# Full-array maxima in the lead, a strip mask made by ScalarE, and narrower score strips in a transformer-block kernel

## The chip, the cores and the metric

The kernel runs on one core of one Trainium2 chip, in one launch. What is measured is the device time of that core in microseconds (us), from the first to the last instruction with what lies around them. The engines in the text are TensorE (PE in the profile, with its weight loads as PEld), VectorE (DVE), ScalarE (ACT), GpSimd (POOL) and the queue that issues most DMAs (SP).

## The reference

A block of a sequence model: layer norm and sliding-window attention, a residual sum, then layer norm and a gated mixer over the sequence, and a second residual sum. Only the attention half is touched here. Sizes are S = 2048 positions, D = 640, 32 heads of 20, and a window of 256 keys.

```
q, k, v = split(layernorm(x) @ wqkv)            # 32 heads, Dh = 20
scores  = q @ k.T * Dh**-0.5
mask    = (i - j >= 0) & (i - j < 256)          # query i, key j
p       = softmax(where(mask, scores, -1e9))
h       = x + (p @ v) @ wo
z       = gelu(layernorm(h) @ w_in); z1, z2 = halves of z
out     = h + (z1 * (w_sp @ layernorm(z2) + b_sp)) @ w_out
```

## The kernel before

Positions are cut into 16 tiles of 128. The kernel runs through these stages, one behind the other:

- **V stage.** For each tile: layer norm of x (statistics on DVE, the variance plus epsilon and its power of -0.5 on POOL, lines 75 and 76, the normalizing on DVE, line 79), transposes on PE (line 394), a split of the result into a rounded high part and the rest, and the product with the weights for v (lines 410 to 412: high by high, high by low, low by high). The weights are split too: high parts by ACT (line 459), low parts by DVE and POOL (line 460).
- **Q/K stage.** 40 items (`qk_item`, 10 weight blocks m by 4 position chunks c), each of 5 steps of 3 matmuls of 512 columns (lines 434 to 436). A finished item is split into three bf16 parts (lines 440 to 443: ACT, DVE, ACT, POOL) and stored. The first 24 items run alone. The other 16, "dense" in the code, are a generator that yields after each step of 3 matmuls.
- **Lead.** The last 48 and more dense steps alternate with `max_item`s of head group 0 and the first of group 1. A `max_item` computes 128 queries by their keys for one head, to find each query's largest score: four matmuls of 32 queries each, side by side in four column strips of the array (line 278), each over its own 288 keys; then DVE adds a mask and takes the maximum (line 284). `strip` is that mask for query tiles from 2 on, the same pattern in each 32 partitions; `mask` serves tiles 0 and 1.
- **Main loop.** 128 units u (8 groups of 4 heads by 16 key tiles), 130 steps. Step s issues, for each of 4 heads hh, the `max_item` of unit s + 20 and the `score_item` of unit s: 128 keys by up to 384 queries, four strips of 32 keys, each over the same 384 queries (line 332), into one of three PSUM banks `s2`; ACT takes the exponential of the whole 128x384 (line 335). Behind hh = 2 comes the `pv_item` of unit s - 2 (line 356), in f32, which first had POOL clear what lies outside the window (lines 337 and 340). Every fourth pv ends with a copy from PSUM by ACT (line 366). At four steps ahead of a new head group `max_rows` sends the maxima through DRAM (m_d, lines 297 and 299) into the rows that the group's first scores read. From unit 109 on there are no maxima left, and scores go two heads at a time into other banks.
- **Mixer.** Output projection, second layer norm and the gated mixer. The diff does not touch it.

PE, DVE and ACT run in the order in which the code is written. POOL and SP are ordered by a scheduler. In the prologue, POOL has to make the constants (`ident`, `half`, `mask`, `strip`, the ones in `v_sb`) and its share of line 460, and between them lies the power that the first normalized tile waits for.

The strip mask is made so before:

```
strip = tmp2.tile([P, 288], BF16, name="strip")
nc.gpsimd.memset(strip, 0.0)
for j in range(4):
    m = strip[32 * j:32 * j + 32]
    nc.gpsimd.affine_select(out=m, ... pattern=[[1, 288]], base=-1, channel_multiplier=-1, ...)
    nc.gpsimd.affine_select(out=m, ... pattern=[[-1, 288]], base=256, channel_multiplier=1, ...)
```

## Time and profile before

| | |
|---|---|
| time, three runs | 1188.43, 1192.71 (median), 1193.15 us |
| the profiled execution's own time | 1185.69 us |
| its span, first to last instruction | 1184.0 us |
| mean granted TensorE clock in it | 0.991 |
| PE busy | 1126.5 us (95%), 10272 matmuls |
| PEld, DVE, ACT, POOL busy | 963.8, 738.8, 537.6, 391.5 us |
| prologue, up to the first v matmul | 12.6 us |
| V stage to about 94 us, Q/K alone to about 196 us, lead to about 265 us, main loop to about 510 us | |

The ends of matmuls are modelled in this profile, so the start times of PE rows carry more than their durations: the distance from one group of matmuls to the next is what PE really took. "xN" merges N instructions of one kind that follow each other. In a row of a timeline the numbers are the start and the length in us; in square brackets stands how long the engine had been idle and what ended that. Rows of line 278 are maxima, of 332 scores, of 356 pv, of 434 to 436 dense Q/K steps.

### The profile page before, as it was taken

What the parts mean: (1) busy time and instruction counts of PE and PEld (TensorE: products, weight loads), DVE (VectorE), ACT (ScalarE), POOL (GpSimd) and SP (SyncE); (2) the same over time, 40 slices, a digit from 0 to 9 for tenths busy, and PEclk for the clock granted to TensorE, in tenths of its full rate; (3) what the DMA queues carried; (4) which work ended last, traced back from release to release, by engine and by line L of the source; (5) the groups of instructions that cost most, each with busy time, mean ns of one, the idle gap of its engine ahead of it and who ended that gap; (6) DMA issues with size and microseconds to landing.
All of it is one profiled execution on the core that took longest, in us unless ns stands there. A gap on an engine that the chain in (4) does not pass through costs nothing. (4 is left out here: it accounts for less than half of the span.)

```text
span 1184.0 us, 26538 instructions
## 1 busy us (share of the span) xinstructions
PE 1126.5 (95%) x10272; PEld 963.8 (81%) x10272; DVE 738.8 (62%) x1949; ACT 537.6 (45%) x1121; POOL 391.5 (33%) x485
## 2 busy tenths in 40 slices
PE   5999999999999999878899999899999899999998
PEld 5998886546666666468899999799999889999998
DVE  5541123658888888559967658755548985656443
ACT  3333433228888888834446655433335531221110
POOL 4123443336556555845722036100015530000000
PEclk9999999999999999989999999899999999999999
DMA  6212453543444441558845441133331364444322
GB/s 191 77 34 89 143 195 138 187 150 114 173 166 175 174 175 42 188 174 289 270 156 189 174 134 36 36 132 131 120 139 57 125 193 152 129 140 136 86 87 82
DMA packets 72125, 165.20 MB, mean 140 GB/s; under 512 B 9128, under 2 KB 33448, under 8 KB 70056
## 3 DMA queue, kind: packets, MB, share of 16 engines
q1 hardware_dynamic: 69696, 158.27, 40.1%
q10 hardware_dynamic: 2304, 5.24, 1.1%
q8 instruction: 80, 1.31, 0.5%
q14 instruction: 45, 0.37, 0.1%
HBM read 108.83 MB, written 54.66 MB: 138 GB/s over the span
## 5 line engine op out<-in xcount | busy, mean ns | idle before, releaser
L335 ACT ACTIVATE pt<-st 128x384 f32<-128x384 f32 (+2 forms) x474 | 199.0, 513 | 34.8 <-PE st L332 27.3
L284 DVE CUSTOM_DVE_ANT_0 junk<-sm,strip 128x288 bf16<-128x288 f32 x448 | 181.0, 454 | 50.8 <-PE sm L278 49.6
L930 PE MATMUL g<-zl,aw 128*128 128x432 f32 x768 | 173.6, 361 | 7.2 <-ACT zl L598 4.9
L598 ACT ACTIVATE aw<-fx 128x512 fp32r<-128x512 f32 (+2 forms) x160 | 92.9, 596 | 185.7 <-PE g L930 120.9
L930 PEld LDWEIGHTS g<-zl,aw 128*128 128x128 f32 x768 | 144.6, 189 | 15.3 <-ACT zl L598 5.7
L930 PE MATMUL g<-ze,aw 128*128 128x432 f32 x576 | 137.0, 365 | 4.1 <-DVE row L592 1.8
L592 DVE TENSOR_TENSOR aw<-fx,aw 128x512 fp32r<-128x512 f32 (+2 forms) x152 | 108.4, 722 | 36.2 <-ACT aw L598 36.0
L930 PEld LDWEIGHTS g<-ze,aw 128*128 128x128 f32 x576 | 108.8, 192 | 11.6 <-ACT aw L598 1.7
L332 PE MATMUL st<-slot 123*32 123x384 bf16 (+2 forms) x1536 | 110.6, 318 | 6.6 <-ACT pt L335 3.6
L337 POOL TENSOR_SCALAR_AFFINE_SELECT pt<-pt 128x512 f32<-128x512 f32 x128 | 82.1, 642 | 90.9 <-ACT pt L335 90.9
L278 PE MATMUL sm<-slot 120*32 120x288 bf16 (+2 forms) x1536 | 109.1, 284 | 3.2 <-DVE mcol L284 2.5
L356 PE MATMUL pv<-pt,v_sb 128*32 128x384 f32 (+2 forms) x1408 | 102.7, 384 | 3.0 <-POOL pt L340 1.9
L969 PE MATMUL out_ps<-wout,y_sp 128*128 128x320 f32 (+1 forms) x630 | 96.2, 309 | 0.4 <-ACT y_sp L122 0.4
L834 PE MATMUL zb<-win,aw 128*128 128x432 f32 x480 | 95.3, 359 | 0.0
L969 PEld LDWEIGHTS out_ps<-wout,y_sp 128*128 128x128 f32 (+1 forms) x630 | 94.1, 188 | 1.2 <-ACT y_sp L122 0.7
L834 PEld LDWEIGHTS zb<-win,aw 128*128 128x128 f32 x480 | 89.9, 187 | 4.7
L278 PEld LDWEIGHTS <-slot 120*32 120x32 bf16 x1536 | 49.2, 95 | 42.6 <-issue 35.0
L332 PEld LDWEIGHTS <-slot 123*32 123x32 bf16 x1536 | 50.4, 96 | 38.3 <-issue 19.3
L441 DVE TENSOR_TENSOR rest<-qk,sg 128x512 f32<-128x512 f32 x40 | 27.7, 691 | 86.3 <-ACT sg L440 86.0
L443 POOL TENSOR_TENSOR sg<-rest,sg 128x512 bf16<-128x512 f32 x40 | 46.5, 1163 | 98.7 <-ACT sg L442 96.2
L340 POOL TENSOR_SCALAR_AFFINE_SELECT pt<-pt 128x512 f32<-128x512 f32 x112 | 73.9, 660 | 0.0
L592 DVE TENSOR_TENSOR row<-g,row 128x432 f32<-128x432 f32 x80 | 48.1, 604 | 36.0 <-PE g L930 32.3
(172 smaller groups left out, 2092.8 us busy)
## 6 DMA issues: line engine op xcount, KB each, us to landing
slot<-qk_d SPq DMA_DIRECT2D x72, 320.0 KB
fx<-wsp_in SPq DMA_DIRECT2D x32, 512.0 KB
qk_d<-sg SPq DMA_DIRECT2D x40, 384.0 KB
fx<-hn_d SPq DMA_DIRECT2D x32, 320.0 KB
o_d<-ot SPq DMA_DIRECT2D x32, 256.0 KB
xb<-qk_d SPq DMA_DIRECT2D x24, 320.0 KB
z_d<-row SPq DMA_DIRECT2D x16, 432.0 KB
g_d<-row SPq DMA_DIRECT2D x16, 432.0 KB
```

The source lines that it names most:

```text
L278: nc.tensor.matmul(ps[32 * j:32 * j + 32, :n], st[:120, 0, hh, q0:q0 + 32], st[:120, 1, hh, k0:k0 + n], start=True, stop=True, tile_positi ...
L284: nc.vector.tensor_tensor_reduce(out=junk[:, :n], in0=ps[:, :n], in1=keep, scale=1.0, scalar=NEG, op0=OP.add, op1=OP.max, accum_out=m_cols ...
L332: nc.tensor.matmul(ps[32 * i:32 * i + 32, j, :n], st[:123, 1, hh + j, k0:k0 + 32], st[:123, 0, hh + j, kb * P:kb * P + n], start=True, sto ...
L335: nc.scalar.activation(pt[:, hh:hh + width, :n], ps[:, :, :n], AF.Exp, scale=SCALE)
L337: nc.gpsimd.affine_select(out=pt[:, :, :P], in_=pt[:, :, :P], pattern=[[0, 4], [1, P]], base=0, channel_multiplier=-1, compare_op=OP.is_ge ...
L340: nc.gpsimd.affine_select(out=pt[:, :, 256:], in_=pt[:, :, 256:], pattern=[[0, 4], [-1, P]], base=-1, channel_multiplier=1, compare_op=OP. ...
L356: nc.tensor.matmul(ps[32 * hh:32 * hh + 32, a - 512 * c:b - 512 * c], v_sb[:, kb, v0:v0 + 32], pt[:, hh, a - kb * P:b - kb * P], start=fir ...
L592: (eng or nc.vector).tensor_tensor(out=out, in0=a, in1=b, op=op)
L598: nc.scalar.activation(out, a, AF.Copy)
L834: nc.tensor.matmul(b[0][:, :HF], a[t][:, x, kk], win2[0][:, y, kk, h * HF:(h + 1) * HF], start=kk + x + y == 0, stop=kk == KD - 1 and x == 1)
L930: nc.tensor.matmul(ps, w[m][:, x, k], zc[k][m][:, y], start=start and k + x + y == 0, stop=stop and k == 3 and x == 1, skip_group_check=True)
L969: nc.tensor.matmul(ps[j][:, :HD], src[:w, a, k, :], e1["wout"][:w, b, k, j * HD:(j + 1) * HD], start=(k == 0 and a + b == 0), stop=(k == K ...
```

## The change

Four things. (1) In the lead, a `max_item` is one matmul of 128 queries by up to 384 keys on the full array, and DVE reduces up to 384 columns with a mask of that width; in the main loop tiles from 2 on keep the strips (tiles 0 and 1 use the full array there too). (2) `mask` has 384 columns and is made by two selects of POOL; the strip mask is no longer made by POOL but copied from `mask` by four ACT instructions at the start of the Q/K stage. (3) A single-head score strip computes the 288 queries that its 32 keys can reach instead of 384; the exponential still reads all 384 columns, in which what a strip didn't write is left from earlier scores and lies where POOL clears it. The three `s2` banks are allocated once and used in turn, by the V stage's transposes too. (4) The splitting of a Q/K item is a generator of its own, advanced after the first and the second step of the next item. `m3` has one buffer instead of two.

```diff
-        mask = tmp2.tile([P, 256], BF16, name="mask")
+        mask = tmp2.tile([P, 384], BF16, name="mask")
         nc.gpsimd.memset(mask, 0.0)
-        nc.gpsimd.affine_select(out=mask, in_=mask, pattern=[[-1, 256]], base=128, channel_multiplier=1,
+        nc.gpsimd.affine_select(out=mask, in_=mask, pattern=[[1, 384]], base=-1, channel_multiplier=-1,
+                                compare_op=OP.is_ge, fill=NEG)
+        nc.gpsimd.affine_select(out=mask, in_=mask, pattern=[[-1, 384]], base=256, channel_multiplier=1,
                                 compare_op=OP.is_ge, fill=NEG)
         strip = tmp2.tile([P, 288], BF16, name="strip")
-        nc.gpsimd.memset(strip, 0.0)
-        for j in range(4):
-            m = strip[32 * j:32 * j + 32]
-            nc.gpsimd.affine_select(out=m, in_=m, pattern=[[1, 288]], base=-1, channel_multiplier=-1,
-                                    compare_op=OP.is_ge, fill=NEG)
-            nc.gpsimd.affine_select(out=m, in_=m, pattern=[[-1, 288]], base=256, channel_multiplier=1,
-                                    compare_op=OP.is_ge, fill=NEG)
...
+        s2s, s2n = [ps6[0].tile([P, 512], F32, name=f"s2_{i}") for i in range(3)], [0]
...
         def s2_tile(name):
-            return ps6[0].tile([P, 512], F32, tag="s2", bufs=3, name=name)
+            s2n[0] += 1
+            return s2s[s2n[0] % 3]
...
-        def max_item(g, qb, hh):
+        def max_item(g, qb, hh, strips=True):
...
-            if qb < 2:
-                n, keep = (qb + 1) * P, mask[:, 256 - (qb + 1) * P:]
+            lo = max(0, qb - 2) * P
+            n = (qb + 1) * P - lo
+            if strips and qb > 1:
+                n, keep = 288, strip
+                for j in range(4):
+                    q0 = qb * P + 32 * j
+                    nc.tensor.matmul(ps[32 * j:32 * j + 32, :n], st[:120, 0, hh, q0:q0 + 32],
+                                     st[:120, 1, hh, lo + 32 * j:lo + 32 * j + n], start=True, stop=True,
+                                     tile_position=(0, 32 * j))
             else:
-                n, keep = 288, strip
-            for j in range(4):
-                q0 = qb * P + 32 * j
-                k0 = 0 if qb < 2 else q0 - 256
-                nc.tensor.matmul(ps[32 * j:32 * j + 32, :n], st[:120, 0, hh, q0:q0 + 32], st[:120, 1, hh, k0:k0 + n],
-                                 start=True, stop=True, tile_position=(0, 32 * j))
+                keep = mask[:, 384 - n:]
+                nc.tensor.matmul(ps[:, :n], st[:120, 0, hh, qb * P:(qb + 1) * P], st[:120, 1, hh, lo:lo + n],
+                                 start=True, stop=True)
...
                 for i in range(4):
                     k0 = kb * P + 32 * i
-                    nc.tensor.matmul(ps[32 * i:32 * i + 32, j, :n], st[:123, 1, hh + j, k0:k0 + 32],
-                                     st[:123, 0, hh + j, kb * P:kb * P + n], start=True, stop=True,
+                    b, e = (32 * i, min(n, 32 * i + 288)) if width == 1 else (0, n)
+                    nc.tensor.matmul(ps[32 * i:32 * i + 32, j, b:e], st[:123, 1, hh + j, k0:k0 + 32],
+                                     st[:123, 0, hh + j, kb * P + b:kb * P + e], start=True, stop=True,
                                      tile_position=(0, 32 * i))
...
                     nc.tensor.matmul(ps, lo[:, k, :], xn_hi[c][:, k, :], start=False, stop=(k == KD - 1))
+                    if k < 2:
+                        next(after[0], None)
                     yield
+                for _ in after[0]:
+                    pass
+                after[0] = split_qk(m, c, ps)
+                next(after[0])
+
+            def split_qk(m, c, ps):
                 sg = tmp.tile([P, 3, 512], BF16, tag="ta", bufs=3, name=f"sg{m}_{c}")
                 rest = tmp.tile([P, 512], F32, tag="tb", bufs=2, name=f"rest{m}_{c}")
                 nc.scalar.activation(sg[:, 0, :], ps, AF.Copy)
+                yield
                 nc.vector.tensor_tensor(out=rest, in0=ps, in1=sg[:, 0, :], op=OP.subtract)
+                yield
                 nc.scalar.activation(sg[:, 1, :], rest, AF.Copy)
...
+            for j in range(4):
+                r = slice(32 * j, 32 * j + 32)
+                nc.scalar.activation(strip[r], mask[r, 32 * j:32 * j + 288], AF.Copy)
...
-                    max_item(0, u, hh)
+                    max_item(0, u, hh, False)
```

Three places show what stands where. First POOL in the prologue, before the first normalized tile; `mva` holds the statistics of a tile (75 and 76 are its epsilon and power), `slot` the split v weights. Before:

```order
L222 AFFINE_SELECT mask<-mask 128x256
L228 AFFINE_SELECT strip<-strip 32x288 x4
L233 MEMSET v_sb 128x16x11
L235 MEMSET v_sb 128x16x32
L230 AFFINE_SELECT strip<-strip 32x288 x3
L75 TENSOR_SCALAR mva_162<-mva_162 128x1
L230 AFFINE_SELECT strip<-strip 32x288
L460 TENSOR_TENSOR slot_96<-wvraw_141,slot_96 128x320
L460 TENSOR_TENSOR slot_96<-wvraw_143,slot_96 128x320
L76 TENSOR_TENSOR mva_162<-mva_162,half 128x1
```

And with the change, where the lines have other numbers (222 and 224 the selects, 474 the weights' low parts):

```order
L228 MEMSET v_sb 128x16x11
L230 MEMSET v_sb 128x16x32
L222 AFFINE_SELECT mask<-mask 128x384
L224 AFFINE_SELECT mask<-mask 128x384
L75 TENSOR_SCALAR mva_143<-mva_143 128x1
L76 TENSOR_TENSOR mva_143<-mva_143,half 128x1
L474 TENSOR_TENSOR slot_96<-wvraw_122,slot_96 128x320
L474 TENSOR_TENSOR slot_96<-wvraw_124,slot_96 128x320
```

The power stood behind eight strip selects and two low parts of the weights; now it stands behind two mask selects and ahead of the low parts.

Second, PE in the lead: one dense step and one maximum (`sm`). Before, in pairs of a weight load and a matmul for each strip:

```order
L434 MATMUL qk_1_1932<-xa,wqh_1687 128x512
L435 MATMUL qk_1_1932<-xa,wqh_1687 128x512
L436 MATMUL qk_1_1932<-xa,wql_1688 128x512
L278 LDWEIGHTS slot_96
L278 MATMUL sm_3_3_1946<-slot_96 32x288
L278 LDWEIGHTS slot_96
L278 MATMUL sm_3_3_1946<-slot_96 32x288
L278 LDWEIGHTS slot_96
L278 MATMUL sm_3_3_1946<-slot_96 32x288
L278 LDWEIGHTS slot_96
L278 MATMUL sm_3_3_1946<-slot_96 32x288
```

With the change (438 to 440 are the dense step, 280 the maximum):

```order
L438 MATMUL qk_1_1839<-xa,wqh_1636 128x512
L439 MATMUL qk_1_1839<-xa,wqh_1636 128x512
L440 MATMUL qk_1_1839<-xa,wql_1637 128x512
L280 LDWEIGHTS slot_96
L280 MATMUL sm_4_1_1865<-slot_96 128x384
```

Four pairs became one, over 384 columns instead of 288; the order of dense steps and maxima is as it was.

Third, PE in the main loop at a step whose maxima are of tile 0 or 1 of a head group, between two groups of scores. Before:

```order
L332 LDWEIGHTS slot_96
L332 MATMUL st_0_3404<-slot_96 32x384
L278 LDWEIGHTS xb
L278 MATMUL sm_0_1_3410<-xb 32x128
L278 LDWEIGHTS xb
L278 MATMUL sm_0_1_3410<-xb 32x128
L278 LDWEIGHTS xb
L278 MATMUL sm_0_1_3410<-xb 32x128
L278 LDWEIGHTS xb
L278 MATMUL sm_0_1_3410<-xb 32x128
L332 LDWEIGHTS slot_96
L332 MATMUL st_1_3417<-slot_96 32x384
```

With the change (336 are the scores, into a fixed bank):

```order
L336 LDWEIGHTS slot_96
L336 MATMUL s_0_112<-slot_96 32x288
L280 LDWEIGHTS xb
L280 MATMUL sm_0_1_3071<-xb 128x128
L336 LDWEIGHTS slot_96
L336 MATMUL s_1_113<-slot_96 32x288
```

A maximum of four strips among groups of four strips became one matmul of the full array among them; of the program's 128 full-array maxima 80 stand in the lead and 48 here, 8 at each of six pairs of steps (units 12 and 13 of head groups 0 to 5). The scores' strips have 288 columns.

On ACT the second part of a Q/K item (line 442 before) now comes behind the high part of the next weight block where one is due, once for each block; on DVE the item's rest (line 441 before) stands between the same two maxima in the lead as it did.

More of the change, by code (lines that the diff above doesn't have):

```diff
@@ L289, in max_rows @@
             nc.tensor.transpose(ps[:64, :P], m_cols.pop(g), ident)
-            m3 = tmp2.tile([64, 3, P], BF16, tag="m3", bufs=2, name=f"m3_{g}")
+            m3 = tmp2.tile([64, 3, P], BF16, tag="m3", bufs=1, name=f"m3_{g}")
             mr = tmp2.tile([64, P], F32, tag="mr", bufs=2, name=f"mr{g}")
@@ L414, in vgemm @@
                                          ps[:, :HD].rearrange("p (h c) -> p h c", c=DH), AF.Copy)
-            wqs, raws = {}, {}
+            wqs, raws, after = {}, {}, [iter(())]
             def load_wqk(m):
@@ L524, in block_kernel @@
                     if u:
-                        max_item(1, u - 1, hh)
+                        max_item(1, u - 1, hh, False)
                     next(dense, None)
             for hh in range(4):
-                max_item(1, LEAD - 17, hh)
+                max_item(1, LEAD - 17, hh, False)
             for _ in dense:
+                pass
+            for _ in after[0]:
                 pass
```

2 lines of the change are left out of this document (1 added, 1 removed).

## Prediction

> **What bounds the kernel now.** I read the busy time by stretches first. PE is busy nearly all the time in the lead and in the main loop, but its ends are modelled, so the table only says where to look.
>
> ```profile
> 194.00:251.00 57.00, 56.42 (x401) 28.99 (x400) 34.10 (x139) 11.68 (x19) 15.13 (x11) 1.00 0.50 173
> 300.00:460.00 160.00, 152.95 (x3541) 102.30 (x3539) 134.24 (x679) 138.07 (x351) 94.43 (x155) 1.00 0.44 160
> ```
>
> So I took the timeline of PE and measured from start to start. In the Q/K stage a dense step takes 0.68 us (160.42 to 161.10), 0.227 a matmul, and the next weights (PEld) load in 0.19 us under the running matmul.
>
> ```profile
> 160.42 0.39 PE L434 MATMUL qk<-xb,wqh 128*128 128x512 f32 x1
> 161.10 0.39 PE L434 MATMUL qk<-xb,wqh 128*128 128x512 f32 x1
> 160.43 0.19 PEld L435 LDWEIGHTS qk<-xb,wqh 128*128 128x128 f32 x1
> ```
>
> In the lead the same step with one maximum in between takes 1.13 us (225.65 to 226.78), and a query tile of three steps and four maxima 3.51 us (227.90 to 231.41).
>
> ```profile
> 225.65 0.31 PE L278 MATMUL sm<-slot 120*32 120x288 bf16 x4
> 226.46 0.39 PE L436 MATMUL qk<-xb,wql 128*128 128x512 f32 x1
> 226.78 0.10 PEld L278 LDWEIGHTS <-slot 120*32 120x32 bf16 x4 [0.36 <-issue]
> 226.78 0.31 PE L278 MATMUL sm<-slot 120*32 120x288 bf16 x4
> 227.01 0.50 PE L434 MATMUL qk<-xb,wqh 128*128 128x512 f32 x1
> ...
> 227.90 0.43 PE L278 MATMUL sm<-slot 120*32 120x288 bf16 x8
> 231.41 0.43 PE L278 MATMUL sm<-slot 120*32 120x288 bf16 x8
> ```
>
> A maximum among dense steps thus costs 1.13 - 0.68 = 0.45 us. The last dense matmul would make room at 226.46 + 0.23 = 226.69; the strips' weights are loaded only at 226.78, after PEld stood idle for 0.36 us, and the dense weights again only when the strips are through. Going to strips and back costs about 0.3 us over what the columns take. That is the lead's bound: PE, with a third of a maximum's time being work.
>
> The main loop is another matter. One step, PE and ACT:
>
> ```profile
> 311.19 0.31 PE L278 MATMUL sm<-xb 120*32 120x288 bf16 x4
> 311.31 0.35 PE L332 MATMUL st<-slot 123*32 123x384 bf16 x4
> 311.48 0.31 PE L278 MATMUL sm<-xb 120*32 120x288 bf16 x4
> 311.71 1.64 ACT L335 ACTIVATE pt<-st 128x384 f32<-128x384 f32 x4 [0.23 <-PE st L332]
> 312.25 0.35 PE L332 MATMUL st<-slot 123*32 123x384 bf16 x4
> 312.42 0.84 PE L356 MATMUL pv<-pt,v_sb 128*32 128x256 f32 x16
> 313.07 0.31 PE L278 MATMUL sm<-xb 120*32 120x288 bf16 x4
> 313.19 0.35 PE L332 MATMUL st<-slot 123*32 123x384 bf16 x4
> 313.59 1.64 ACT L335 ACTIVATE pt<-st 128x384 f32<-128x384 f32 x4 [0.24 <-PE st L332]
> ```
>
> PE alone needs 0.125 us for a group of maxima (311.19 to 311.31), 0.165 for a group of scores (to 311.48) and 0.65 for the pv (312.42 to 313.07): 4 x 0.29 + 0.65 = 1.81 us. The step is 1.88 (ACT's row at 311.71 to that at 313.59). What closes it is a ring through the three score banks: ACT's first exponential starts at 311.71, and 0.54 later the scores at 312.25 have the bank that it freed (PE's maxima before them, not shown, would have let them start some 0.06 earlier); then come those scores (0.165), the pv (0.65), a group of maxima (0.125), the last scores of the step at 313.19 and, 0.40 us after their start, ACT's next first exponential. 0.54 + 0.17 + 0.65 + 0.12 + 0.40 = 1.88. ACT is idle 0.24 us in every round and still belongs to the bound.
>
> **The change, part by part.** The sum goes against the profiled execution's 1185.69 us.
>
> *Prologue.* POOL's strip mask stands ahead of the first tile's normalizing:
>
> ```profile
> 4.06 0.21 DVE L74 BATCH_NORM_AGGREGATE mva<-sta 128x2 f32<-128x12 f32 x1
> 5.46 1.51 POOL L230 TENSOR_SCALAR_AFFINE_SELECT strip<-strip 32x288 bf16<-32x288 bf16 x3
> 5.48 0.74 DVE L460 TENSOR_TENSOR slot<-wvraw,slot 128x320 fp32r<-128x320 f32 x1 [1.22 <-ACT slot L459]
> 7.30 0.47 ACT L459 ACTIVATE slot<-wvraw 128x320 fp32r<-128x320 f32 x1 [0.59 <-DMA wvraw<-wv_in]
> 7.87 1.67 POOL L460 TENSOR_TENSOR slot<-wvraw,slot 128x320 fp32r<-128x320 f32 x2
> 9.50 0.57 POOL L76 TENSOR_TENSOR mva<-mva,half 128x1 f32<-128x1 f32 x1
> 10.11 0.61 DVE L79 TENSOR_SCALAR xn<-xt,mva 128x640 f32<-128x640 f32 x1 [3.88 <-POOL mva L76]
> 12.58 0.63 PE L410 MATMUL v<-slot,xa 128*128 128x320 f32 x1 [0.47 <-ACT xa L398]
> ```
>
> The statistics are done at 4.27; the power that needs them ends at 10.07. With the strips gone and the power ahead of the weights' low parts, POOL is free by about 4.3 and the power ends near 5.2; DVE then still has its first weight part until 6.22 and normalizes there, 3.9 us earlier. The high parts on ACT (last at 7.30 to 7.77, set by a DMA) come next: the transposes of the tile end at about 8.0, so ACT is free for them. First v matmul at 12.58 - 3.9 = 8.7: **-3.9 us**. Bounds: -2 if the second half of the weights lands too late, -4.5. The strip copies on ACT (four of 32x288, each no longer than the 0.47 us of a 128x320 copy, 1.9 together) lie ahead of the first item's split, under an item's 15 x 0.227 = 3.4 us of matmuls: 0; without that cover 1.9.
>
> *Lead.* The full-array maximum has 384 columns, as the score groups have, so I take their 0.17 us, and no going back and forth. A query tile then takes 3 x 0.68 + 4 x 0.17 = 2.72 instead of 3.51: 16 x 0.79 = 12.6. The eight maxima of group 1 that still lie between dense steps have 128 and 256 columns:
>
> ```profile
> 252.83 0.24 PE L278 MATMUL sm<-slot 120*32 120x128 bf16 x4
> 253.89 0.24 PE L278 MATMUL sm<-slot 120*32 120x128 bf16 x4
> ```
>
> 1.06 against 0.68 + 0.17: 8 x 0.21 = 1.7. Together **-14.3**. DVE has to keep up; a reduction grows with its columns:
>
> ```profile
> L284 DVE CUSTOM_DVE_ANT_0 junk<-sm,strip 128x288 bf16<-128x288 f32 x286 | 114.2, 454 | 22.4 <-PE sm L278 21.3
> L284 DVE CUSTOM_DVE_ANT_0 junk<-sm,mask 128x128 bf16<-128x128 f32 x22 | 5.5, 282 | 0.0
> ```
>
> (454 - 282) / 160 = 1.08 ns a column, so 384 columns take 0.56, and one follows the other every 0.38 + 0.10 = 0.48 us (0.38 is the distance of two now: 114.2 us over 286 rows is 0.40). 4 x 0.48 with a share of the items' rests is 2.3 of the 2.72 us: not the bound, though near. Bounds of a full-array maximum: 0.16 (nothing but columns) and 0.36, if its own 0.19 us of weight load lies open too.
>
> [...]
>
> *Behind the lead.* Eight maxima follow the last dense step with nothing between them, paced by DVE: 8 x 0.10 = 0.8 us later. It is mostly covered, since ACT's first exponential waits for POOL anyway:
>
> ```profile
> 266.50 4.32 ACT L335 ACTIVATE pt<-st 128x384 f32<-128x384 f32 x11 [2.77 <-POOL sg L443]
> ```
>
> I take **+0.3** (0 to 0.8).
>
> *Main loop, narrower scores.* 97 single-head units have all 384 queries (14 of 16 in six groups, 13 in the last). 96 columns less shorten a group by 0.165 - 0.125 = 0.04. In the ring this counts twice, in the scores before the pv and in the start of the exponential behind the last scores: 0.08 a step, not the 0.16 that PE saves. The exponential is as wide as before. At every fourth step ACT's copy of the pv stands between, and the step is 2.02 long:
>
> ```profile
> 314.13 0.35 PE L332 MATMUL st<-slot 123*32 123x384 bf16 x4
> 315.09 0.63 ACT L366 ACTIVATE ot<-pv 128x512 f32<-128x512 f32 x1
> 316.15 0.35 PE L332 MATMUL st<-slot 123*32 123x384 bf16 x4
> ```
>
> There the exponential waits for the copy, not for the last scores, so only 0.04 counts: 21 such steps. 76 x 0.08 + 21 x 0.04 = **-6.9**. Bounds: 0 and -15.5 (97 x 0.16). Three fixed banks in turn are what three buffers were: 0.
>
> *Main loop, full-array maxima.* Tiles 0 and 1 of groups 2 to 7 are now full-array matmuls among strips, 48 in all. None is in this trace; the nearest is the lead's island of the other kind, at 0.3 us over its columns. 48 x 0.30 = +14.4. They fall where PE already waits:
>
> ```profile
> PE sm L278 <- DVE mcol L284: 2.1, 6, 0.4
> PE st L332 <- DMA slot<-m_d: 2.1, 3, 1.1
> PE st L332 <- DMA xb<-m_d: 0.5, 1, 0.5
> ```
>
> Between 270 and 480 us PE waits 2.1 us for DVE, which is then busy with `max_rows`, and 2.6 us for the maxima's trip through DRAM; slower PE work in between takes the place of both: 14.4 - 2.1 - 2.6 = **+9.7**. Bounds: 0 (only the 0.09 us of going in, which the waits cover) and +15 or more.
>
> *Deferred splitting.* The order on DVE is the same; on ACT a weight block's high part goes ahead of one second part, once a block. PE has no gap in that stage and two banks for it: 0. Should PE wait for it after all, it would be one such copy a block, 640 columns at the 0.47 us for 320: 6 x 0.9, some 5 us.
>
> Sum: -3.9 - 14.3 + 0.3 - 6.9 + 9.7 = **-15.1**, 1185.7 - 15.1 = 1170.6 for a profiled execution. The three timed runs lie 3 to 7 us above it; the middle of all four is 1190.6, and 1190.6 - 15.1 gives **1175 us**. What can be told from no change is about 0.5%, 6 us.
>
> **The rivals.**
>
> *Switches inside the main loop are cheap* (10%). For: the islands' neighbours are strips with 0.1 us of weights. Against: PEld's 0.36 us of idleness in the lead. Then +9.7 becomes 0: -24.8, 1166.
>
> *The main loop follows PE's columns* (8%). For: PE busy 152.95 of 160. Against: the ring above. -15.5 instead of -6.9: -23.7, 1167.
>
> *The narrower scores do not shorten the step* (8%), so that the change does not do there what it says. For: the exponential is as wide as ever and ACT is in the ring. Against: the scores are in it too. -8.2: 1182.
>
> *The lead keeps its price* (9%): full-array weights lie open, 0.36 us a maximum: 16 x (3.51 - 3.48) + 8 x 0.02, about 0.7 instead of 14.3. -1.5: 1189, no change. [...]
>
> *Slower* (5%): each of the 48 islands also throws the ring of banks out of step, because the scores behind it start late and their exponential with them; a second 0.3 for the switch and 0.3 for the ring make 0.9 each, 43.2 instead of 14.4 us, +13.7: 1204. For: both sides of an island are scores that the ring needs. Against: in those steps the maxima are of 128 and 256 columns, and PE has some 0.3 us to spare. It decides from 0.61 us an island, where 48 x 0.61 equals all that is gained or covered (29.5).
>
> **How the numbers follow.** The forecast has 60%, with 1168 to 1182 of its own. From the cheap switches to the lead that keeps its price would be 1166 to 1189; cutting the latter and adding the bounds of prologue and lead gives 1163 to 1186 for 8 in 10. Faster by over 0.5%: 0.60 + 0.10 + 0.08 and half of the 8%, 0.82; within 0.5%: the 9% and some of that 8%, 0.12; slower 0.06.
>
> **What would show it.** First v matmul near 8.7 us. A lead tile near 2.7 us with no idle time of PEld before a maximum; 3.5 there would be the exposed load. Common steps of the main loop 1.80 us apart; 1.72 would be PE's columns, 1.88 no gain. At units 12 and 13 of a group some 2 us more than now, and the waits on m_d gone. I am wrong if the exponentials end the gain, if the islands cost 0 or 0.6, or if a DMA holds the prologue.

## The result, and the profile after

The changed kernel takes **1172.44 us** in the median of four runs (1171.26 to 1176.24), the kernel before in the runs beside it 1191.55 us (1188.43 to 1193.15): a ratio of 0.985, 95% interval 0.982 to 0.988. A second set of six runs against eleven (the ninth experiment) gave 1173.18 against 1184.65 us, 0.989 (0.987 to 0.992). So the gain is 12 to 20 us, about 15, against 15.1 forecast. The two traces differ by only 9.8 us, because the profiled execution of before was faster than its timed runs and that of the changed kernel slower. By stretches, each from a first row to a first row:

| us | before | after | difference | forecast |
|---|---|---|---|---|
| up to the first v matmul | 12.58 | 8.98 | -3.6 | -3.9 |
| V stage | 82.7 | 82.5 | -0.2 | 0 |
| Q/K stage | 98.0 | 97.0 | -1.0 | 0 |
| lead | 68.0 | 56.4 | -11.6 | -14.3 |
| last dense matmul to first exponential | 5.30 | 7.11 | +1.8 | +0.3 |
| first exponential to last window mask | 240.8 | 243.5 | +2.8 | -6.9 + 9.7 |
| mixer | 676.7 | 678.7 | +2.0 | 0 |

The mixer's code is the same. Among the experiments below, which do not touch it either, it takes 675 to 680 us, so its 2.0 can't be told from chance. The sum was right to a few tenths of a per cent; two of its terms were wrong and cancel others. In the row from the first exponential to the last window mask forecast and measurement agree to the digit, and that is luck: the +9.7 did not come, and late instructions and a halved clock, shown below, filled its place.

**Prologue.** The timeline of the changed kernel, all engines:

```profile
4.70 0.57 POOL L76 TENSOR_TENSOR mva<-mva,half 128x1 f32<-128x1 f32 x1
...
5.74 0.61 DVE L79 TENSOR_SCALAR xn<-xt,mva 128x640 f32<-128x640 f32 x1
...
7.97 0.47 ACT L473 ACTIVATE slot<-wvraw 128x320 fp32r<-128x320 f32 x1 [0.95 <-DMA wvraw<-wv_in]
8.35 0.74 ACT L402 ACTIVATE xa<-s 128x512 fp32r<-128x512 f32 x2
...
8.98 0.64 PE L414 MATMUL v<-slot,xa 128*128 128x320 f32 x1 [1.26 <-ACT xa L402]
```

The power stands ahead of the weights' low parts and the tile is normalized at 5.74 instead of 10.11. What ends last now is a DMA: ACT waits 0.95 us for the fifth block of weights (the row at 7.97), and the copy of the transposed tile stands behind it.

**Lead.** PE's timeline:

```profile
213.97 0.34 PE L280 MATMUL sm<-slot 120*128 120x384 bf16 x1
...
214.62 0.40 PE L440 MATMUL qk<-xb,wql 128*128 128x512 f32 x1
214.85 0.34 PE L280 MATMUL sm<-slot 120*128 120x384 bf16 x1
214.90 0.53 PE L438 MATMUL qk<-xb,wqh 128*128 128x512 f32 x1
...
218.54 0.50 PE L280 MATMUL sm<-slot 120*128 120x384 bf16 x2
...
221.35 0.50 PE L280 MATMUL sm<-slot 120*128 120x384 bf16 x2
```

A dense step with a maximum takes 0.88 us (213.97 to 214.85), the maximum 0.88 - 0.68 = 0.20, a query tile 2.81 (218.54 to 221.35; 3.51 before). But the lead has two stalls that before did not have, of 0.49 and 1.27 us. The first of them, all engines:

```profile
222.00 0.60 ACT L452 ACTIVATE sg<-qk 128x512 bf16<-128x512 f32 x1 [3.58 <-DMA qk_d<-sg]
...
222.70 0.69 DVE L454 TENSOR_TENSOR rest<-qk,sg 128x512 f32<-128x512 f32 x1 [1.29 <-ACT sg L452]
...
223.92 0.32 PE L280 MATMUL sm<-slot 120*128 120x384 bf16 x1 [0.49 <-DVE mcol L286]
```

ACT's copy of a finished item waits for its buffer, that is for the store of the item three back; DVE's subtraction waits for the copy, the reductions stand behind the subtraction, and PE waits for the reductions.

**Behind the lead.** Timeline, then the granted clock (the eighth column) in stretches of 2 us:

```profile
244.83 0.40 PE L440 MATMUL qk<-xb,wql 128*128 128x512 f32 x1
...
249.27 0.69 DVE L454 TENSOR_TENSOR rest<-qk,sg 128x512 f32<-128x512 f32 x1
...
250.75 1.15 POOL L457 TENSOR_TENSOR sg<-rest,sg 128x512 bf16<-128x512 f32 x1 [1.90 <-ACT sg L456]
...
251.93 4.87 ACT L339 ACTIVATE pt<-s 128x384 f32<-128x384 f32 x11 [1.32 <-POOL sg L457]
252.47 0.43 PE L336 MATMUL s<-slot 123*32 123x288 bf16 x4 [1.79 <-ACT pt L339]
```

```profile
250.00:252.00 2.00, 0.31 (x4) 0.10 (x4) 1.46 (x8) 0.68 (x2) 1.15 (x1) 0.86 0.57 168
252.00:254.00 2.00, 1.53 (x28) 1.20 (x31) 0.79 (x3) 2.00 (x6) 0.30 (x1) 0.50 0.72 265
...
258.00:260.00 2.00, 2.00 (x55) 1.42 (x48) 1.74 (x9) 1.78 (x5) 1.22 (x2) 0.93 0.71 269
```

The last item's deferred subtraction now stands on DVE behind all eight last maxima, at 249.27, 4.4 us behind the last dense matmul. The third part on POOL and the first exponential, which takes over that memory, are late with it. PE waits 1.79 us and is granted half the clock for 6.8 us (0.86, 0.50, 0.50, 0.50 and 0.93 in the five stretches from 250 to 260), and the first two steps, taken from one step's first window mask on POOL to the next, last 1.73 and 3.20 us instead of 1.47 and 1.87. The way and the clock cost about 1.8 + 1.6 us. The clock fell at about 251.4 (from the 0.86), when a wait of 0.55 us and 0.8 us of the 1.79 had passed, with 0.31 us of work between them.

**Main loop.** One round of PE and ACT:

```profile
320.72 1.64 ACT L339 ACTIVATE pt<-s 128x384 f32<-128x384 f32 x4 [0.15 <-PE s L336]
...
321.26 0.31 PE L336 MATMUL s<-xb 123*32 123x288 bf16 x4
321.39 0.83 PE L360 MATMUL pv<-pt,v_sb 128*32 128x384 f32 x8
322.03 0.31 PE L275 MATMUL sm<-slot 120*32 120x288 bf16 x4
322.16 0.31 PE L336 MATMUL s<-xb 123*32 123x288 bf16 x4
...
322.51 1.64 ACT L339 ACTIVATE pt<-s 128x384 f32<-128x384 f32 x4 [0.15 <-PE s L336]
```

0.54 to the scores that get the freed bank, then 0.13, 0.64 and 0.13, and 0.35 from the last scores to the next exponential: 1.79 us, the forecast's ring with its 1.80. The fourth steps stay at 2.02. The steps with full-array maxima:

```profile
400.53 0.31 PE L336 MATMUL s<-slot 123*32 123x288 bf16 x4
400.77 0.23 PE L280 MATMUL sm<-slot 120*128 120x128 bf16 x1
400.93 0.31 PE L336 MATMUL s<-slot 123*32 123x288 bf16 x4
```

From scores to scores takes 0.40 us around such a maximum, of which the step feels little: the four steps of a group around the two that hold eight of them took 7.46 us together, mask to mask, and take 8.02 now, 0.57 more. The step behind, which waited for m_d before, is 0.57 shorter (2.41 in the mean to 1.84).

What nobody expected stands in rows like these, the first at a fourth step, where the loop loses over a microsecond at once:

```profile
292.63 0.84 PE L360 MATMUL pv<-pt,v_sb 128*32 128x128 f32 x16
294.51 0.31 PE L275 MATMUL sm<-xb 120*32 120x288 bf16 x4 [1.04 <-issue]
...
300.98 0.31 PE L275 MATMUL sm<-xb 120*32 120x288 bf16 x4 [0.91 <-DVE mcol L286]
```

"issue" means that the profile shows nothing that PE waited for; in the second row it names DVE, whose last such read had ended at 300.04. Four such stalls, 0.75 to 1.57 us, add up to 4.3.

### The profile page after: what moved, and what is told of

Its sections match the earlier page's. It is cut to its first block, busy times and chain, and to the rows that moved or that the text cites. A ratio compares the mean times of both kernels' runs of the same rounds, so it can differ in the third digit from the quotient of the medians.

```text
span 1174.2 us, 25759 instructions
## 1 busy us (share of the span) xinstructions
PE 1116.0 (95%) x9888; PEld 961.9 (82%) x9888; DVE 744.1 (63%) x1949; ACT 543.1 (46%) x1125; POOL 388.8 (33%) x477
## 5 line engine op out<-in xcount | busy, mean ns | idle before, releaser
L339 ACT ACTIVATE pt<-s 128x384 f32<-128x384 f32 (+2 forms) x436 | 175.9, 488 | 27.2 <-PE s L336 18.6
L286 DVE CUSTOM_DVE_ANT_0 junk<-sm,strip 128x288 bf16<-128x288 f32 x384 | 153.4, 454 | 30.0 <-PE sm L275 27.3
L341 POOL TENSOR_SCALAR_AFFINE_SELECT pt<-pt 128x512 f32<-128x512 f32 x128 | 82.5, 645 | 93.6 <-ACT pt L339 93.5
L336 PE MATMUL s<-slot 123*32 123x288 bf16 (+5 forms) x1232 | 87.7, 288 | 3.7 <-ACT pt L339 3.2
L275 PE MATMUL sm<-slot 120*32 120x288 bf16 x1088 | 77.5, 294 | 1.3 <-DVE mcol L286 0.7
L286 DVE CUSTOM_DVE_ANT_0 junk<-sm,mask 128x384 bf16<-128x384 f32 (+2 forms) x128 | 54.9, 454 | 14.1 <-PE sm L280 13.5
```

What stands on the lines that cost most here:

```text
L275: nc.tensor.matmul(ps[32 * j:32 * j + 32, :n], st[:120, 0, hh, q0:q0 + 32], st[:120, 1, hh, lo + 32 * j:lo + 32 * j + n], start=True, stop ...
L286: nc.vector.tensor_tensor_reduce(out=junk[:, :n], in0=ps[:, :n], in1=keep, scale=1.0, scalar=NEG, op0=OP.add, op1=OP.max, accum_out=m_cols ...
L336: nc.tensor.matmul(ps[32 * i:32 * i + 32, j, b:e], st[:123, 1, hh + j, k0:k0 + 32], st[:123, 0, hh + j, kb * P + b:kb * P + e], start=True ...
L339: nc.scalar.activation(pt[:, hh:hh + width, :n], ps[:, :, :n], AF.Exp, scale=SCALE)
L341: nc.gpsimd.affine_select(out=pt[:, :, :P], in_=pt[:, :, :P], pattern=[[0, 4], [1, P]], base=0, channel_multiplier=-1, compare_op=OP.is_ge ...
```

## The experiments

Each is timed against the kernel before on its own chip. Those of one set (1 to 4, 5 to 8, 9 to 11, 12) share its runs. Nothing is left out of the computation in any of them.

**1. The narrower scores alone**, in the kernel before, with the three fixed banks that they need:

```diff
-                    nc.tensor.matmul(ps[32 * i:32 * i + 32, j, :n], ...
+                    b, e = (32 * i, min(n, 32 * i + 288)) if width == 1 else (0, n)
+                    nc.tensor.matmul(ps[32 * i:32 * i + 32, j, b:e], ...
```

> The kernel before with one part of the change: each strip of one head's score tile computes only the 288 queries that its window can reach, in three fixed banks. Everything else, the strip maxima, the mask built at the start, the splitting, is as before. My theory (a ring of three score tiles, each released by an exponential that reads a tile just as long as before, sets a step of four heads): the common step of the main loop goes from 1.87 us to about 1.80 us, the prologue, the lead and the way to the first exponential stay as they were, and the kernel gets 5 to 7 us faster, about 1185 us against 1191.6. Rival 1 (the loop follows the columns of TensorE): the common step goes to about 1.72 us and the kernel gets about 15 us faster, 1177 us. Rival 2 (the exponentials and the masks alone set the step): the step stays 1.87 us and the time stays at 1191.6 us within 2 us.

Measured: 1182.11 against 1187.9 us, ratio 0.9949 (0.9933 to 0.9966), 6.1 us less. The common step is 1.79 us, the fourth step 2.02. The ring holds; neither PE's columns (1.72) nor the exponential alone (1.87) set the step.

**2. Strips again for tiles 0 and 1 of the main loop**, in the changed kernel:

```diff
-                nc.tensor.matmul(ps[:, :n], st[:120, 0, hh, qb * P:(qb + 1) * P], ...
+                for j in range(4 if strips else 1):
+                    r = slice(32 * j, 32 * j + 32) if strips else slice(0, P)
+                    nc.tensor.matmul(ps[r, :n], ...
```

> The changed kernel, but in the main loop the maxima of query tiles 0 and 1 are four strips each again, with the same mask and the same width as in the changed kernel; the lead keeps full-array maxima. My prediction priced the 48 full-array maxima of the main loop at +0.30 us each, 9.7 us net of two waits that they remove: by it this kernel takes about 1163 us. The traces read since say otherwise: the steps that hold the full-array maxima are 0.58 us longer a group and the step with the wait on the store of the maxima is 0.57 us shorter a group, so that by them this kernel takes 1172 us within 2 us, with the step around units 11 to 13 back at some 1.9 and 2.3 us and the step with the wait back at about 2.4 us. A third theory, that the full-array maxima are what makes the irregular stalls of the main loop (4 to 5 us in the profiled execution of the changed kernel), gives about 1168 us and a trace without those stalls.

Measured: 1171.53 us, ratio 0.9862 (0.9838 to 0.9885), the changed kernel's time within the interval. PE in one of these steps:

```profile
398.07 0.24 PE L282 MATMUL sm<-slot 120*32 120x128 bf16 x4
398.13 0.31 PE L339 MATMUL s<-slot 123*32 123x288 bf16 x4
398.25 0.24 PE L282 MATMUL sm<-slot 120*32 120x128 bf16 x4
```

Here a maximum and its scores take 0.18 us (398.07 to 398.25), against 0.40. The four steps are 0.6 us shorter a group (7.40), as the trace had it, and 9.7 us are refuted. One part of the expectation failed: the wait for m_d did not come back to 2.4 us; four of its six steps stay at 1.84 and one has 3.71. So the narrower scores and not only the full-array maxima had shortened it (the first experiment has 1.84 to 2.56 there). Set against these strips, the 48 full-array maxima cost 6 x 0.62 = 3.7 us in the trace and give back 2.2 at m_d; what remains, some 1.5 us, is too little for the total to show. Of stalls ahead of maxima two are left, so the full-array maxima do not make them.

**3. Splitting at once**, in the changed kernel:

```diff
-                    if k < 2:
-                        next(after[0], None)
...
-                after[0] = split_qk(m, c, ps)
-                next(after[0])
+                for _ in split_qk(m, c, ps):
+                    pass
```

> The changed kernel, but every Q/K item is split as soon as it is finished, as in the kernel before. My prediction gave the deferral nothing in either direction. Reading the traces: the way from the last dense matmul to the first exponential goes from 7.1 us back to about 5.3 us, the clock granted around the first score steps goes back to 1.00 (another 1.5 us), and the Q/K stage takes back about 1 us, in all 2 to 3 us less, about 1170 us. Rival 1 (the deferral is what shortened the lead by keeping the wait on the ScalarE copy off VectorE's queue): the lead gets 3 us or more longer, its maxima wait behind the splitting, and the kernel takes 1174 us or more. Rival 2 (nothing of it decides): 1172.4 us within 1 us.

Measured: 1171.77 us, ratio 0.9855 (0.9829 to 0.9881). The trace does what was read: 5.30 us to the first exponential, clock 1.00 in all stretches, first steps 1.47 and 1.79. The Q/K stage takes 98.1 and the lead 57.6 us; in the second profiled execution of the changed kernel (experiment 9) they take 98.2 and 57.8. So the deferral brings neither stage anything and costs what stands behind them, but the total does not show these 3 us: the profiled execution took 1165.58 us, the other five 1170.47 to 1172.98, as the changed kernel does, and why is open.

**4. Only the last item split at once:**

```diff
-                    next(dense, None)
+                    if next(dense, "end") == "end":
+                        for _ in after[0]:
+                            pass
```

> The changed kernel, but the last Q/K item of the lead is split right behind its last matmul, ahead of the last eight maxima in VectorE's queue; all other items stay deferred. My reading (the last item's subtraction behind eight maxima holds back the store of Q and K and so the end of the lead): the way from the last dense matmul to the first exponential goes from 7.1 us to 5.3 us, no drop of the granted clock to 0.50 behind it, and the kernel gets 2 to 3.5 us faster, about 1169.5 us. Rival (the first exponential waits for something else that ends at nearly the same time, a load of the stack or a mask of POOL): the subtraction comes earlier and the first exponential does not; 1172.4 us within 1 us.

Measured: 1171.5 us, ratio 0.9856 (0.9831 to 0.9881). The way is 5.30 us, and the first steps are 1.85 and 1.79, better than 1.73 and 3.20. But the clock still drops, for 3.4 us by these two stretches:

```profile
254.00:256.00 2.00, 1.91 (x36) 1.35 (x35) 2.00 (x12) 1.35 (x4) 0.61 (x1) 0.61 0.42 106
256.00:258.00 2.00, 2.00 (x41) 1.58 (x36) 1.95 (x11) 2.00 (x5) 1.24 (x2) 0.54 0.87 258
```

And in this execution the lead is 59.5 us long, with stalls of 1.17 and 2.07. The expected drop of the total did not appear.

**5. The lead and the masks alone**, without narrower scores, deferral and the main loop's full-array maxima: the edits of 2 and 3 and

```diff
         def s2_tile(name):
-            s2n[0] += 1
-            return s2s[s2n[0] % 3]
+            return ps6[0].tile([P, 512], F32, tag="s2", bufs=3, name=name)
...
+                    b, e = 0, n
```

> The kernel before with two parts of the change: the mask and its strip copy (built by three instructions of POOL and four copies of ScalarE), and full-array maxima in the lead. Scores, splitting and the main loop's strip maxima are those of before. By the traces: first v matmul at 9.0 us instead of 12.6 us (3.6 us less), lead 11 to 12 us shorter, way to the first exponential 5.3 us as before, in all 14 to 16 us less or a ratio near 0.987. My prediction's own price of these two parts was 3.9 + 14.3 = 18.2 us, a ratio of 0.985. Rival (the deferred splitting is what lets the lead run so fast): the lead is only 5 to 8 us shorter and the ratio is 0.990 or more.

Measured: 1171.53 against 1187.32 us, ratio 0.9869 (0.9851 to 0.9888), 15.5 us: the larger part of all that the change brings. First v matmul at 9.12, lead 56.8 us with stalls of 0.69 and 1.50, 5.30 us to the first exponential. With the 6.1 us of experiment 1 the two parts would make 21.6; the changed kernel shows 12 to 20. Its traces have three things that take from it: the way and the clock behind the lead (3.4 us), the full-array maxima of the main loop, and more of the late blocks that experiment 6 is about.

**6. The stack loads in halves**, in the changed kernel:

```diff
-                    src = qk_d[..., g % 4 * 4:g % 4 * 4 + 4]
-                    nc.sync.dma_start(st[j:6 * DH:6, a], src)
+                    for h in (0, 2):
+                        src = qk_d[..., g % 4 * 4 + h:g % 4 * 4 + h + 2]
+                        nc.sync.dma_start(st[j:6 * DH:6, a, h:h + 2], src)
```

> The changed kernel, but each load of the stacked Q and K is issued as two of half the size (two heads each, 20 rows of 8 KB instead of 20 rows of 16 KB), so that SP's own issue time of about 0.7 us each keeps fewer bytes waiting at the DMA engines. Theory from the trace: the irregular stalls of TensorE in the main loop (0.75 to 1.6 us, four in the changed kernel's profiled execution) are blocks of 256 TensorE instructions that land late, because their fetch stands up to 4 us behind these loads; every such stall ends about 1.5 us after a block has landed. If so, the fetches come within 2 us of the block before, the stalls are gone, and the kernel takes 3 to 5 us less, 1168 us against 1172.4 us. Rival 1 (the fetch waits for bytes on a shared engine, not for what is queued): stalls as before, 1172 us within 1.5 us. Rival 2 (twice the issues hold back the stores and the maxima on SP's queue): the waits on the stores grow and the kernel takes 1175 us or more.

Measured: 1180.71 us, ratio 0.9948 (0.993 to 0.9966), some 8 us slower than the changed kernel, and yet the first theory holds. None of the irregular stalls is left: from the third step on the common steps are 1.79 to 1.80 and the fourth ones 2.02 throughout, but for a 2.25 and a pair of 2.08 and 1.50 that nearly all runs have at the same place. When PE's blocks of instructions landed is taken from the trace's DMA records (us):

```
                     fetch starts, lands       PE goes on       behind the landing
changed kernel       292.00, 292.96            294.51           1.55
                     298.51, 299.38            300.98           1.60
                     387.46, 388.47            390.08           1.61
                     394.29, 395.30            396.82           1.52
distances from one fetch to the next, from 282.8 on:
changed kernel       9.2, 6.5, 3.7
halved loads         6.0, 5.8, 5.6
```

The stalls of a pair are 256 rows of PE apart, matmuls and weight loads counted. With halved loads the steps run at the same pace while the loads are under way, so it is not a slower loop that leaves the fetches more time. And the lead, by stretches of this kernel and of the changed one, has lost its two stalls as well:

```profile
190.76:245.10 54.34, 53.68 (x254) 34.35 (x253) 43.55 (x159) 14.73 (x24) 17.50 (x14) 1.00 0.53 192
```

```profile
188.43:244.83 56.40, 53.99 (x254) 34.52 (x253) 43.07 (x159) 14.73 (x24) 17.53 (x14) 1.00 0.52 191
```

What costs the 8 us is the second rival, with another wait: SP is busy issuing 24 loads until 303.0 (12 until 293.8 in the changed kernel), the last rows land at 305.96, and the next group's first maximum waits for them, 0.95 to 2.63 us in five groups. SP's queue and PE:

```profile
282.84 5.25 SPq L263 DMA_DIRECT2D slot<-qk_d  x7
288.19 0.41 SPq L374 DMA_DIRECT2D o_d<-ot  x1
288.64 9.47 SPq L263 DMA_DIRECT2D slot<-qk_d  x12
298.22 0.41 SPq L374 DMA_DIRECT2D o_d<-ot  x1
298.68 4.32 SPq L263 DMA_DIRECT2D slot<-qk_d  x5
```

```profile
306.57 0.22 PE L281 MATMUL sm<-slot 120*128 120x128 bf16 x1 [1.75 <-DMA o_d<-ot]
```

The waits are not the whole of it. In the longest one, 2.63 us up to 339.75, the granted clock falls to one half and stays there to about 349.6; behind the one that ends at 375.6 it is halved for another 3.4 us:

```profile
340.00:342.00 2.00, 2.00 (x24) 0.78 (x27) 1.19 (x7) 1.15 (x3) 0.00 (x0) 0.50 0.00 0
...
348.00:350.00 2.00, 2.00 (x37) 1.59 (x31) 1.33 (x6) 1.34 (x4) 1.22 (x2) 0.59 0.22 75
```

**7. The stores of Q and K on ScalarE's queue:**

```diff
-                nc.sync.dma_start(bass.AP(tensor=base.tensor, ...
+                nc.scalar.dma_start(bass.AP(tensor=base.tensor, ...
```

> The changed kernel, but the store of every split Q/K item is issued by ScalarE on its own DMA queue instead of by SP behind the stack loads. Theory: the lead's two stalls of TensorE (0.49 and 1.27 us in the changed kernel, up to 2.07 us in the runs so far) are a ScalarE copy that waits for its buffer's old store, and that store stands behind the twelve plus six stack loads on SP's queue; on a queue of its own it lands earlier, the two stalls vanish and the lead is about 2 us shorter, 1170.5 us. Rival 1 (the stores share the bytes of the DMA engines whatever the queue): the stalls stay, 1172.4 us within 1 us. Rival 2 (ScalarE has to wait for POOL's third part before it can issue the store, and its next copy stands behind that): the Q/K stage and the lead get longer, 1175 us or more.

Measured: 1194.73 us, ratio 1.0072 (1.0051 to 1.0094): the second rival. ACT and its queue in the Q/K stage, which takes 111.4 us:

```profile
132.56 1.17 POOL L457 TENSOR_TENSOR sg<-rest,sg 128x512 bf16<-128x512 f32 x1
...
133.76 0.37 ACTq L460 DMA_DIRECT2D qk_d<-sg  x1
...
134.23 0.60 ACT L452 ACTIVATE sg<-qk 128x512 bf16<-128x512 f32 x1 [2.44 <-POOL sg L457]
```

ACT stands idle for 2.44 us until POOL's part is there and the store is issued, and only then copies the next item. It says nothing on the first theory.

**8. Four banks for the scores, two for the maxima:**

```diff
-        s2s, s2n = [... for i in range(3)], [0]
+        s2s, s2n = [... for i in range(4)], [0]
-            return ps6[0].tile([P, 512], F32, tag="s1", bufs=3, name=name)
+            return ps6[0].tile([P, 512], F32, tag="s1", bufs=2, name=name)
...
```

> The changed kernel with four fixed banks for the scores and two for the maxima instead of three and three. If the ring of three score banks sets the common step (my theory), a fourth bank lets it fall below 1.79 us to what comes next: TensorE's columns at about 1.72 us, or ScalarE at four exponentials of 0.42 us, 1.70 us; over some 80 common steps 5 to 7 us less, 1166 us. If the two banks left for the maxima become the ring instead (a maximum of VectorE lasts 0.45 us and is followed by a read of 0.08 us), the step grows to 1.9 us or more, the lead too, and the kernel takes 1185 us or more, and TensorE's idle time stands ahead of the strip maxima. If neither ring matters, 1.79 us and 1172.4 us.

Measured: 1197.12 us, ratio 1.0085 (1.0065 to 1.0104), common step 2.15 us. It is the maxima's ring that binds now:

```profile
329.92 0.31 PE L275 MATMUL sm<-slot 120*32 120x288 bf16 x4 [0.19 <-DVE mcol L286]
...
332.07 0.31 PE L275 MATMUL sm<-slot 120*32 120x288 bf16 x4 [0.19 <-DVE mcol L286]
```

Three and three is the better division of the six. What a fourth bank for the scores would bring with three for the maxima was not tried.

**9. The changed kernel again.**

> The changed kernel once more, unaltered, beside the two that follow and beside the kernel before, so that all stand against the same runs. From the first four runs its ratio is 0.985 within 0.003; the profiled execution should show irregular stalls of TensorE ahead of some maxima in the main loop again, 0.5 to 1.6 us each, each about 1.5 us behind the landing of a block of 256 TensorE instructions, and two stalls of 0.5 to 2 us in the lead.

Measured: 1173.18 against 1184.65 us, ratio 0.9891 (0.9866 to 0.9916). Three stalls in the main loop (1.28, 0.67 and 1.30 us), 1.3 to 1.6 us behind a block's landing, and 1.85 and 1.30 us in the lead.

**10. The last item split at once, and halves for fewer loads:**

```diff
+                    step = 2 if g < 3 or j < 3 else 4
+                    for h in range(0, 4, step):
...
```

> The changed kernel with two edits: the last Q/K item is split right behind its last matmul, and the loads of the Q/K stacks are halved as in the run with all halves, but from group 3 on only the first six of twelve, so that SP's queue ends some 2 us earlier than there. Theory: the lead keeps the 54.3 us that it had with all loads halved (56.4 in the changed kernel), the way to the first exponential is 5.3 us instead of 7.1 without the drop of the clock behind it (3.4 us together), the late instruction blocks mostly go, and the wait for the late stack at the end of each load is below 0.5 us a group: about 1165 us on the scale of the first runs, ratio 0.978. Rival (the loads end too late again): a step of 3 us or more where the next group's maxima begin, and 1172 us or more.

Measured: 1169.25 us, ratio 0.986 (0.9834 to 0.9885), 3.9 us below experiment 9 in the mean (1.1 to 6.7, resampling the runs of both). Lead 54.35 us, way 5.29, no stall on a block; but four of the six groups wait for their stack, two of them for 2.02 and 1.67 us, and behind these two the clock is halved again (0.984 in the mean of the execution, 0.991 in that of experiment 11). The rival held half.

**11. The last item split at once, and Q and K in one load for two heads:**

```diff
...
+                        src = bass.AP(tensor=base.tensor, offset=base.offset,
+                                      ap=[[R, DH], [((parts[1] - parts[0]) * 2 * DH + DH) * R, 2],
+                                          [S // 2, 2], [1, S // 2]])
+                        nc.sync.dma_start(st[j:6 * DH:6, :, h:h + 2], src)
```

> The changed kernel with the last Q/K item split right behind its last matmul, and eight of the twelve loads of each stack issued as Q and K together for two heads (40 rows of 8 KB instead of 20 rows of 16 KB): as many issues on SP and as many bytes as in the changed kernel, but shorter rows, and twice as many of them a load. If the rows then spread over all 16 DMA engines instead of 10 (the DMA share during the loads is 0.63 now), the loads end 3 to 5 us earlier, the fetches of instructions wait less, no wait at the next group's first maxima appears, and the kernel takes about 1163 us, ratio 0.977. Rival (the rows stay on 10 engines): the DMA share stays 0.63 during the loads, the late blocks are as frequent as in the changed kernel, and only the last item's split counts: 1169 us.

Measured: 1169.15 us, ratio 0.9862 (0.9838 to 0.9885), 3.6 us below experiment 9 in the mean (1.1 to 6.2). The loads do not spread: the DMA share in the loads' stretches is 0.68 to 0.69. Two stalls of 0.48 and 0.59 us on blocks are left, and no group waits over 0.4 us for its stack. The Q/K stage lost 2.1 us to two stalls, which the halves do not have.

**12. Both:** halves for groups 0 to 2, pairs from group 3 on, the last item split at once.

> The two loads that did best apart, together: the changed kernel with the last Q/K item split right behind its last matmul, the stacks of groups 0 to 2 loaded as halves of one operand (20 rows of 8 KB, as in the run with half loads up to group 3) and those of groups 3 to 7 mostly as Q and K together for two heads (as in the run with pairs). Sum from the two traces: Q/K stage 97.0 us and lead 54.4 us as with the halves (99.6 and 54.9 with the pairs), way to the first exponential 5.3 us, main loop as with the pairs (about 30.4 us a group). That is some 3 us less than the run with pairs (1169.2 us, ratio 0.986): 1166 us, ratio 0.9835 against the kernel before. If only the last split counts, or the halves cost in SP's queue what they save, 1169 us or more.

Measured: **1165.48 us** (1165.09 to 1167.32) against 1186.78, ratio 0.9826 (0.9804 to 0.9849). All five runs lie below all ten of the changed kernel (1170.92 and more), which were timed in other sets. Q/K stage, lead and main loop:

```profile
91.43:188.39 96.96, 96.96 (x422) 78.69 (x421) 18.68 (x27) 39.53 (x66) 45.59 (x35) 1.00 0.45 156
188.39:242.74 54.35, 53.69 (x253) 34.36 (x253) 43.55 (x159) 14.74 (x24) 17.52 (x14) 1.00 0.53 191
248.04:487.09 239.05, 227.49 (x5019) 143.59 (x5014) 189.12 (x906) 211.08 (x502) 150.14 (x239) 1.00 0.44 153
```

The main loop still has two stalls on blocks (0.49 and 1.02 us). This version is faster than the kernel before. Beside the changed kernel it was not timed: by the ratios to the kernel before it stands at 0.983 (0.980 to 0.985) against 0.985 (0.982 to 0.988) and 0.989 (0.987 to 0.992), likely but not shown to be faster than that one.

## Why the prediction was right, and where its steps were wrong

**The whole.** 1175 us was forecast and 1172.4 measured. It was right by two terms that hold (prologue and lead, 15.5 us in experiment 5 where the forecast had 18.2) and one that holds in its mechanism (scores). The term of +9.7 was wrong, and what filled its place had not been thought of: that the total came so close is in part luck.

**Prologue**, -3.9: -3.6. The mechanism is right. The tile is normalized 0.5 us earlier than forecast (5.74, not 6.22), and the DMA of the weights, whose late end was given as the bound of -2, takes back 0.8. A DMA that holds the prologue stood among the signs of being wrong; it does hold it, at a net cost of 0.3.

**Lead**, -14.3: -11.6 and -10.2 in the two executions of the changed kernel, -13.6 where its stalls are gone (experiments 6, 10 and 12). The maximum was mis-sized by 0.03 us (0.17 taken, 0.20 measured). What the step lacked is the items' stores: a shorter lead needs them sooner, and they stand among the stack loads. That the loads are what holds them is shown by experiment 6; that it is SP's order and not the DMA engines' work was meant for experiment 7, which could not tell. The rival with the weight load lying open fell: 0.88 us a step, where it would have been 1.04.

**Behind the lead**, +0.3, and **deferred splitting**, 0: +1.8, and about 1.6 more by the clock. The step that failed is the sentence that the order on DVE is the same. It is for 39 items; the last has no next item, and its subtraction went behind the eight maxima that I had just counted there. Experiment 3 takes it back.

**Narrower scores**, -6.9: -6.1 (interval 4.0 to 8.0) alone. The common step fell by 0.08 as derived. At the fourth steps nothing came of the 0.04: 2.02 in both.

**Full-array maxima in the main loop**, +9.7: about 0 net against before in the trace (+0.57 and -0.57 a group), some +1.5 against the strips of experiment 2, which finds no difference in the total. The term mis-sized is the 0.30 us an island, carried over from the lead. Between scores PE spends 0.40 us around a full-array maximum where strips took 0.18 in experiment 2, 0.22 more, and the step feels 0.57 / 8 = 0.07 of it, because in these steps, with maxima of 128 and 256 columns, PE is ahead of the ring. That is the rival with cheap switches, to which I gave 10%, and by the prediction's own sign (islands that cost 0) this step was wrong. The rival's 1166 us did not come about: the late blocks (4.3), the way and the clock behind the lead (3.4, with 0.3 forecast) and the lead's stalls (2.7 short of the forecast) took the place. Set beside the 0.07, the 0.22 us show that a price on PE need not be one on the loop; what PE spends them on is not shown.

**What was missing**: blocks of instructions that land late, 4.3 and 3.2 us in the two profiled executions of the changed kernel. Before has a narrow escape (a block that landed 1.47 us ahead of its use at 340.96) and one late block, in the middle of a pv:

```profile
432.75 0.51 PE L356 MATMUL pv<-pt,v_sb 128*32 128x384 f32 x1 [0.34 <-issue]
```

The block had landed at 431.31, 1.44 us earlier, and the step lasts 2.71 us instead of 1.87. Whether the change made them more frequent is not shown: the kernel of experiment 1, whose instructions are as many as before, has at least two, and executions differ.

## What to carry to other kernels

When a unit of work is moved behind another in an engine's queue, look at the last one of the series: it has no successor to hide behind, and what it delays is the next stage (by 1.8 us here). A price measured in a stage that PE bounds is not the price in a stage that a ring of banks bounds: the 0.30 us an island, taken from the lead, came to 0.07 in the main loop's step, where only what lies in the ring counted. And when a tuned loop shows stalls that nothing explains, compare their distance in instructions and the landing of instruction blocks: here large loads issued in a burst held up the program itself, by 0.75 to 1.57 us at four places of the main loop, and with these loads in halves none of the four was left.

## What the runs showed of the hardware that I had not expected

Instruction fetch was what TensorE waited for in places, 0.75 to 1.57 us at a time in the changed kernel's main loop. The row of the changed kernel's DMA queues:

```profile
q8 instruction: 77, 1.26, 0.5%
```

77 packets of 16 KB; TensorE's instructions are 2 x 9888 = 19776, which is 77 blocks of 256 and a rest. In nine of the fourteen profiled executions 23 stalls of 0.48 to 1.6 us, shorter ones left aside, end 1.3 to 1.6 us behind the landing of such a block; the profile names nothing for them, or a reduction or a mask that had ended before. In the main loop the fetch of a block normally starts within 2 us of PE's reaching the place, 256 rows earlier, that the block before was needed at (269.51 reached, 270.58 fetched), and some 4 us later while the stack loads run (288.05 reached, 292.00 fetched). When these two fetches start, PE has less than one block left to run. The delay of 3.95 us, 0.96 to the landing and the 1.55 behind it make 6.46 us, and PE takes some 6 us for a block (5.6 to 6.0 from one fetch to the next with halved loads): there is then no reserve. Why the fetch waits, for the number of rows ahead of it on a DMA engine or for their length, is open: halves of 8 KB a row end the stalls, but they also stretch the issue.

In the lead a full-array weight load cost little between matmuls on the same rows: 0.20 us for 384 columns and its weights, with 0.28 us in which PEld stood idle ahead of it. And TensorE's clock was halved for 6.8 us after some 1.3 us of waiting within 1.6 us, and in experiment 4 for 3.4 us after stretches in which PE, paced by DVE, was busy for 0.82 and 1.38 of 2 us with no wait over 0.84 us. Experiment 3 has waits of the same length at the same place (busy for 0.72 and 1.49 of 2 us) and no drop, so what decides is open. In the clock records of the two traces before and after the change the half lasts 3.41, 6.83 or 10.24 us, but for the last one of a kernel, which ends with it.
